# A fused attention and spectral mixer on one Trainium2 core: the last chunk's queries in two halves, one head of its last pack moved to ScalarE, chunk 13 normalised by block transposes

## The chip, the core and the metric

The kernel runs on one core of one Trainium2 chip. The metric is device time of one execution in microseconds (us); the time of a version is the median of its runs. The engines are TensorE (PE in the profile), VectorE (DVE), ScalarE (ACT), GpSimd (POOL) and SyncE (SP, which here only issues transfers).

## What is computed

The input `x` has 2048 tokens of 448 features. Two branches are mixed by a gate per token:

```python
g = sigmoid((x * gate_w).sum(-1, keepdims=True))
# a: attention with 16 heads of 28 features
q, k, v = split(x @ wqkv)
p = softmax(q k^T * 28 ** -0.5)
a = (p v, heads joined) @ wo
# b: spectral filter
b = irfft2(rfft2(x) * (w_r + 1j * w_i))
return g * a + (1 - g) * b
```

All tensors are bfloat16; the output is 2048 x 448.

## The kernel before

**Chunks and tiles.** Attention is worked off in 16 chunks, numbered `c`: four groups of four heads (`T = c // 4`) times four blocks of 512 queries (`qc = c % 4`). Chunk 15 is the last. A chunk has 16 key blocks of 128 keys, so it has 16 x 4 = 64 score pieces of 128 keys x 512 queries, and the whole kernel has 1024. TensorE makes a score piece in one of four strips of 32 rows, one strip per head (`score`, L820). Most pieces go to ScalarE, which takes the exponent of two or three at a time (`exp`, L1053; widths 1024 and 1536, in turns) into a tile `Pt`. The others go to VectorE in packs of one key block with four heads: `pack_step` (L834) writes each head as an integer, and `chain` (L849 to L883) makes the exponent of the four with six or seven further instructions. The seventh (L883) is used when the result is wanted soon; otherwise GpSimd issues a transfer that adds (L878).

**Values.** `pv` (L974) multiplies the exponents with the values of a key block: four TensorE matmuls side by side in four strips of 32 columns, accumulated over the 16 key blocks in one PSUM bank, `psPV`. The values carry a column of ones, so row 28 of each strip holds the softmax sum.

**Closing a chunk.** `close_chunk` takes `psPV` out. For chunks 0 to 13 VectorE copies it (L927), the sums go through four kinds of small transfers and back (L929, L942, L951), and GpSimd multiplies (L963). Chunks 14 and 15 use `turned` instead, on VectorE alone: a transpose in blocks of 32 x 32 (L1434), a reciprocal of the sums (L1435), a product with the gate (L1436), a product with the exponent sums' inverses (L1439) and a transpose back (L1441) into `oT`, from which TensorE takes the output projection. For chunk 15 the last two run twice, for the first and the second 256 queries.

**Output.** A token tile `t` has 128 tokens. `out_unit` (L769, L773) adds the spectral branch and the four groups of heads in a bank for the tiles 0 to 11; a copy (L779) and a transfer (L780) follow. Tiles 12 to 15 are the queries of chunks 3, 7, 11 and 15; all of them but chunk 15's part is made early (`base_unit`) and kept in fp32 (`late`). `finale` then adds chunk 15's part: for tiles 13 and 15 TensorE first loads the kept part into the bank by a product with an identity (fp32, L1457) and ScalarE copies the sum out (L1469), for tiles 12 and 14 VectorE adds it (`add_base`, L814). Four transfers write them (L815, L1470).

**Order.** Each engine works its own queue in the order in which the program issues; semaphores connect the queues. That order is made while the program is built, by a planner in `stream`: for each tile `k` of ScalarE it issues the exponent, then values that are ready (`do_pv`), then other TensorE work (`pick`, `step`), and then the scores of tile `k + 2`, all by estimated clocks for each engine (`tp` for TensorE, `tv` for VectorE, `ta` for ScalarE). `claim` decides which key blocks go to VectorE, `next_tile` what ScalarE gets. Where TensorE would have too little work, `until` and `dummy` put matmuls on zeros (`one_zero`, L1255; `zeros`, L1010). After the last exponent `tail` issues what is left, and `finale` the end.

Of the kernel before, what the change touches and what calls it, by code (L numbers as in the profile page):

```python
# [55 lines left out]
CLAIM, LAST = 10, 5  # L56
FIRST = 3
SOON = 18.1
STEPS, THIN = 3400, 3300
NV, NBASE = 10, 12  # L60
MOST = 7
LATE, LATE_END = 4, 5
BEGIN = 30.0
# [89 lines left out]
class Kernel:  # L153
# [19 lines left out]
    def setup(self):  # L173
# [77 lines left out]
        self.g32 = small("g32", [P, 2, NT], F32)  # L251
# [249 lines left out]
    def gate_unit(self):  # L501
# [21 lines left out]
        def ve(ps):  # L523
            nc.vector.tensor_copy(out=gT[:], in_=ps[0:2 * NT, 0:P])
            nc.vector.tensor_copy(out=gTb[:], in_=gT[:])
            nc.sync.dma_start(out=self.gD[:], in_=gT[0:NT])
            nc.sync.dma_start(out=self.hD[:], in_=gTb[NT:2 * NT])

            gv = self.gD[:]
            for h in range(4):  # L530
                nc.sync.dma_start(out=self.g16[32 * h:32 * h + 32, :, :],
                                  in_=_AP(tensor=gv.tensor, offset=gv.offset, ap=[[16, 32], [QW, 4], [1, 16]]))

            for h in range(4):
                nc.sync.dma_start(out=self.g32[32 * h:32 * h + 32, :, :],
                                  in_=_AP(tensor=gv.tensor, offset=gv.offset + 2 * QW, ap=[[1, 32], [QW, 2], [32, 16]]))
# [268 lines left out]
    def fin_unit(self, t):  # L805

        def ve(ps):
            self.add_base(ps, t, self.nc.sync)
        return Unit(f"fin{t}", [(lambda ps: self.out_pe(ps, t, (3,)), 0.30, 448, ve, 0.54)],
                    needs=[f"base{t}", f"oT{NC - 4 + t // 4}"])  # L810

# [6 lines left out]
    def score(self, out, c, i, h):  # L818
        T, qc = divmod(c, 4)
        self.nc.tensor.matmul(out, lhsT=self.kT[T][32 * h:32 * h + 32, 128 * i:128 * i + 128],  # L820
                              rhs=self.qT[T][32 * h:32 * h + 32, QW * qc:QW * qc + QW],
                              start=True, stop=True, tile_position=(32 * h, 0))

    def pack(self, c, i):

        return {"c": c, "i": i, "left": [0, 1, 2, 3], "t": None}
# [13 lines left out]
    def chain(self, c, i, t):  # L840
# [5 lines left out]

        def o1():
            st["n"] = self.rot1.tile([P, 4, QW], U16, name="n16")
            v.tensor_scalar(out=st["n"][:], in0=t[:], scalar1=511, scalar2=None, op0=ALU.bitwise_and)  # L849

        def o2():
            v.tensor_scalar(out=t[:], in0=t[:], scalar1=127 << 9, scalar2=2, op0=ALU.bitwise_and,  # L852
                            op1=ALU.logical_shift_right)

        def o3():
            st["a"] = self.rot2.tile([P, 4, QW], F16, name="pa16")
            v.tensor_scalar(out=st["a"][:], in0=st["n"][:], scalar1=C3 * k * k, scalar2=C2 * k,  # L857
                            op0=ALU.mult, op1=ALU.add)

        def o4():  # L860
            v.tensor_tensor(out=st["a"][:], in0=st["a"][:], in1=st["n"][:], op=ALU.mult)  # L861

        def o5():
            v.tensor_scalar(out=st["a"][:], in0=st["a"][:], scalar1=0.25 * k, scalar2=0.25 * (C1 * k + 1.0),  # L864
                            op0=ALU.mult, op1=ALU.add)

        soon = self.due(c) < SOON

        def done(at):
            self.pieces[(c, i)] = [t[:, h, :].bitcast(BF16) for h in range(4)]  # L870
            self.pack_t[(c, i)] = at

        def o6():
            q = st["a"][:] if soon else st["a"][:].bitcast(U16)
            v.tensor_tensor(out=q, in0=st["a"][:], in1=st["n"][:], op=ALU.mult)  # L875
            if not soon:

                nc.gpsimd.dma_start(out=t[:], in_=q, accum_op=ALU.add)  # L878
# [3 lines left out]
        def o7():  # L882
            v.tensor_tensor(out=t[:], in0=t[:], in1=st["a"][:], op=ALU.add)  # L883
            done(self.tv + VP + READY)
        for fn, cost, of in ((o1, E_TS, st), (o2, E_TS, None), (o3, E_TS, st), (o4, E_TT, st), (o5, E_TS, st),
                             (o6, E_TT, st)) + ((o7, E_TT, st),) * soon:
            self.vq.append((fn, cost, of))

    def due(self, c):

        return 4 * 0.447 * sum(len(self.free[n]) for n in range(self.act_c, c + 1) if n < NC)
# [23 lines left out]
    def close_chunk(self, c):  # L915
# [3 lines left out]
        if c == NC - 2:  # L919
            f = self.rot2.tile([P, NT, 32], F32, name="ot", tag="o32")  # L920
            z = self.rot2.tile([P, NT, 32], BF16, name="oz", tag="sqh")
            for part in self.turned(c, f, z, (0,)):
                self.dve(part)
# [32 lines left out]
        def scale():  # L956
            if c == 12:
                assert all(n in self.marks for n in ("k3.3", "q3.3", "f1.15"))
                self.oT.append(self.per.tile([P, S], BF16, name="oT3", tag="xT_oT3"))
# [9 lines left out]
    def pv(self, c, i, first, last):  # L969
        T = c // 4  # L970
        pcs = self.pieces.pop((c, i))
        self.packs -= self.pack_t[(c, i)] is not None
        for h in range(4):
# [69 lines left out]
    def exp(self, k):  # L1043
# [10 lines left out]
        for e, (c, i, h) in enumerate(self.tiles[k]):  # L1054
            self.pieces.setdefault((c, i), [None] * 4)[h] = Pt[:, e, :]
            if h == 3:
# [3 lines left out]
    def plan(self):  # L1060
        self.free = {c: list(range(NT)) for c in range(NC)}
        self.act_c, self.act_h, self.act_i = 0, 0, None
        self.epk = None
# [31 lines left out]
        m += [(0.0, self.out_unit(t)) for t in range(NBASE)] + [(0.0, self.fin_unit(t)) for t in range(NBASE, 12)]  # L1095
        self.mand = m

    def claim(self):
# [4 lines left out]
        for c, least in ((self.act_c + 1, NT - 4), (self.act_c, (LAST if self.act_c == NC - 1 else CLAIM) if self.act_c else FIRST)):  # L1103
# [4 lines left out]
            if len(self.free[c]) >= least and self.has(needs):  # L1108
                self.packs += 1
                return self.pack(c, self.free[c].pop(at))  # L1110

    def next_tile(self, k):

        t = []
        while len(t) < (2 if k % 2 else 3) and self.act_c < NC:
            if self.act_i is None:
                if not self.free[self.act_c]:
                    self.act_c += 1
                    continue
                self.act_i = self.free[self.act_c].pop(0)  # L1120
            t.append((self.act_c, self.act_i, self.act_h))
            assert self.act_c > 3 or {f"q0.{self.act_c}", f"k0.{self.act_i // 4}"} <= self.marks.keys()
            self.act_h = (self.act_h + 1) % 4
# [19 lines left out]
    def pick(self):  # L1143
# [6 lines left out]
        if banks:  # L1150
# [6 lines left out]
            for t, u in self.mand[-16:]:  # L1157
                if u.name[0:3] in ("out", "fin") and self.has(u.needs):
# [46 lines left out]
    def small(self, limit):  # L1205

        b = [i for i in (0, 1) if i not in self.open and self.bank_free[i] <= self.tp + 0.1]
        for _, u in self.mand:
            if b and u.name[0:3] == "fin" and self.has(u.needs):
                return self.step(u, b[0], limit)  # L1210
        return False

# [40 lines left out]
    def one_zero(self):  # L1253
        if self.pv_open:
# [4 lines left out]
        elif self.pv_c < NC and 2 not in self.open and self.tp >= self.pv_free:  # L1259
# [8 lines left out]
    def until(self, at):  # L1268

        while self.tp + E_MM <= at and self.thin(at) and self.one_zero():  # L1270
# [17 lines left out]
    def stream(self):  # L1288
# [4 lines left out]
        self.dummies = self.owed = 0  # L1293
        self.pv_c, self.pv_free, self.pv_open = 0, 0.0, False
# [18 lines left out]
        while self.ring:  # L1313
# [15 lines left out]
            while True:  # L1329
# [12 lines left out]
                if u is None or not self.step(*u, limit) and not self.small(limit):  # L1342
# [11 lines left out]
    def do_pv(self, k, left, most):  # L1354
        done = 0
        while done < most and self.pv_c < NC:
            c = self.pv_c
            if self.tp < self.pv_free or 2 in self.open:
                break
            cand = None  # L1360
            for i in sorted(left[c]):
                if not self.has([f"W{i // 4}" if c < 4 else f"V{i}"]):
                    continue
                if (c, i) not in self.pack_t:
                    continue
                t = self.pack_t[(c, i)]
                if t is None:
# [10 lines left out]
            first = len(left[c]) == NT  # L1378
            left[c].discard(cand)
            last = not left[c]  # L1380
            self.pv(c, cand, first, last)
# [4 lines left out]
            if last:  # L1386
                self.dve(0.75 if c == NC - 2 else 0.60, at=self.tp + PV)
# [5 lines left out]
                break  # L1393


    def tail(self):
# [8 lines left out]
        rest = sorted(left[c])  # L1405
        for i in rest:
            if i in rest[1:2]:

                for b, (u, _) in list(self.open.items()):
                    if len(u.phases) > 1:  # L1410
                        self.step(u, b, 1e9)
            self.pv(c, i, len(rest) == NT and i == rest[0], i == rest[-1])
        self.copy = nc.scalar.copy
        while self.open or len(self.mand) > 2 or any(u.name[0:3] != "fin" for _, u in self.mand):
            t = self.ready()
            assert t < 1e8, self.mand[0][1].name
            self.tp = max(self.tp, t)
            u = self.pick()
            if u:
                self.step(*u, 1e9)  # L1420
            else:
                self.tp += 0.2
            self.run_events()
        self.rest = [int(u.name[3:]) for _, u in self.mand]
        self.tail_left = [u.name for _, u in self.mand]

    def turned(self, c, f, z, parts):
# [4 lines left out]
        n = NT // len(parts)  # L1432
        i16 = self.rot2.tile([P, NT], F32, name="i16")
        v.transpose(out=f[:].rearrange("p j r -> p (j r)"), in_=self.psPV[:])  # L1434
        v.reciprocal(out=i16[:], in_=f[:, :, DH])  # L1435
        v.tensor_tensor(out=i16[:], in0=i16[:], in1=self.g32[:, qc - 2, :], op=ALU.mult)  # L1436
        for a in parts:
            zh = z[:, a:a + n, :]
            v.tensor_tensor(out=zh, in0=f[:, a:a + n, :], in1=with_free(i16[:, a:a + n], [[1, n], [0, 32]]), op=ALU.mult)  # L1439
            at = QW * qc + 32 * a  # L1440
            v.transpose(out=self.oT[T][:, at:at + 32 * n], in_=zh.rearrange("p j r -> p (j r)"))  # L1441
            yield 1.95

    def finale(self, psp):


        nc = self.nc
        v = nc.vector
        T, qc = divmod(NC - 1, 4)
        r = {n: psp.tile([P, n, QW], F32, name=f"ps{n}", tag=f"ps{n}", bufs=1) for n in ((3, 2) if self.N % 2 else (2, 3))}  # L1450
        bg = [psp.tile([P, QW], F32, name=f"bg{b}", tag=f"bg{b}", bufs=1) for b in (0, 1)]
        pf = [bg[0], r[3][:, 0], bg[1], r[2][:, 0]]
        eye = self.Fc[:, P + 8:P + 8 + P]
        for t, ps in zip(self.rest, (r[3][:, 1], r[2][:, 1])):
            self.out_pe(ps, t, (3,))
        for e in (1, 3):
            nc.tensor.matmul(pf[e][:, 0:D], lhsT=eye, rhs=self.base[4 * qc + e], start=True, stop=False)  # L1457
# [74 lines left out]
```

## Time and profile before

| | us |
|---|---|
| median of 3 runs (427.12 to 427.52) | 427.48 |
| the profiled execution, its own time | 426.82 |
| its span in the profile | 425.0 |
| busy: TensorE, ScalarE, VectorE | 408.4, 411.0, 395.3 |
| granted TensorE clock, mean | 1.0 |
| end of ScalarE's last exponent (L1053) | 417.07 |
| end of VectorE's last pack (L883) | 417.06 |
| issue of the last output transfers (L815, SyncE) | 421.72 to 422.59 |

The span runs from the first to the last instruction of the profiled execution; 1.82 us of its time lie around the span, and the median of the runs is 0.66 us above it. Times in a trace are counted from the span's start. In a row of the timeline the first number is the start, the second the length of the merged group; in a row of the chain of waits they are start and length of a step; in a row of the groups the busy time and the mean of one stand behind the bar.

### The profile page before, as it was taken

To read this page: it belongs to the slowest core of one execution; us is meant where nothing else is said; L and a number is where in the kernel's file an instruction comes from. 1 tells how busy PE (TensorE), PEld (TensorE's weight loads), DVE (VectorE), ACT (ScalarE), POOL (GpSimd) and SP (SyncE) were. 2 spreads that over 40 slices of the span, in tenths; PEclk is the share of its full clock that TensorE was granted. 3 is DMA by queue.
4 is the path that set the end of the run, shared out by engine and by line. 5 is a ranking of instruction groups with operands and counts; after the bars stand their busy time and mean duration, and the time that the engine had idled before them with its cause. 6 is when DMAs were issued, how large, how long until landed. Compare 5 with 4: busy or idle time off the path is not lost.

```text
span 425.0 us, 8196 instructions
## 1 busy us (share of the span) xinstructions
PE 408.4 (96%) x3139; PEld 144.9 (34%) x3139; DVE 395.3 (93%) x643; ACT 411.0 (97%) x369; POOL 50.3 (12%) x57
## 2 busy tenths in 40 slices
PE   9999999999999999999999999999999899999996
PEld 5343233333333333333333333333343233222331
DVE  6669889999989999999999999999999999999996
ACT  4999999999999999999999999999999999999994
POOL 6000002020110112011220100102002011201000
PEclk9999999999999999999999999999999999999999
DMA  9900200232302153375664446526453305240242
GB/s 242 211 11 2 7 27 13 64 60 43 77 15 47 24 97 62 74 166 103 159 148 95 104 103 134 96 68 110 108 149 77 76 2 106 54 107 29 57 99 75
DMA packets 30967, 35.08 MB, mean 83 GB/s; under 512 B 13296, under 2 KB 23536, under 8 KB 30896
## 3 DMA queue, kind: packets, MB, share of 16 engines
q1 hardware_dynamic: 26432, 20.48, 20.4%
q0 software_dynamic: 3744, 13.63, 17.5%
q8 instruction: 24, 0.39, 0.4%
q10 hardware_dynamic: 752, 0.44, 0.4%
q14 instruction: 15, 0.12, 0.1%
HBM read 15.10 MB, written 1.96 MB: 40 GB/s over the span
## 4 chain that ended last, share of the span: by engine, by line
PE 45%; ACT 25%; DVE 22%; issue 7%; ACTq 0%; DVEq 0%
ACT Pt L1053 21%; PE psPV L974 8%; PE ps L820 7%; DVE Pd L834 5%; PE bg L820 4%; PE psPV L1255 3%; PE bg L280 3%; PE bg L1010 3%; DVE pa L875 2%; PE bg L769 2%; PE bg L773 2%; DVE n L849 2%; DVE Pd L852 2%; DVE pa L861 2%; ACT early L1053 2%
## 5 line engine op out<-in xcount | busy, mean ns | idle before, releaser
L1053 ACT ACTIVATE Pt<-ps 128x1536 bf16<-128x1536 f32 x339 | 385.9, 1305 | 1.5 <-PE ps L820 0.6
L820 PE MATMUL ps<-qT,kT 32*128 32x512 bf16 x892 | 143.2, 382 | 4.3 <-ACT Pt L1053 2.8
L834 DVE TENSOR_SCALAR Pd<-bg 128x512 uint16<-128x512 f32 x132 | 90.0, 682 | 6.0 <-PE ps L820 4.2
L974 PE MATMUL psPV<-Pt,vsb 128*32 128x512 bf16 x832 | 81.1, 388 | 0.0
L820 PEld LDWEIGHTS <-kT 32*128 32x128 bf16 x1024 | 44.7, 91 | 95.1 <-issue 90.0
L820 PE MATMUL bg<-qT,kT 32*128 32x512 bf16 x132 | 50.6, 383 | 0.8 <-DVE Pd L834 0.3
L878 POOL DMA_DIRECT2D Pd<-pa x26 | 24.0, 924 | 214.7 <-PE ps L820 108.8
L1255 PE MATMUL psPV<-warm 128*128 128x512 bf16 x129 | 41.5, 385 | 0.0
L875 DVE TENSOR_TENSOR pa<-pa,n 128x2048 uint16<-128x2048 f16 (+1 forms) x33 | 40.9, 1240 | 0.5
L861 DVE TENSOR_TENSOR pa<-pa,n 128x2048 f16<-128x2048 f16 x33 | 40.9, 1239 | 0.3
L974 PEld LDWEIGHTS <-vsb 128*32 128x32 bf16 x1024 | 23.4, 93 | 52.0 <-issue 51.5
L1010 PE MATMUL bg<-warm 32*128 32x512 bf16 x92 | 35.2, 383 | 1.9 <-DVE Pd L834 1.8
L963 POOL TENSOR_TENSOR oT<-o,rep 128x512 bf16<-128x512 f32 x14 | 17.7, 1264 | 144.5 <-DVE oT L962 77.3
L280 PE MATMUL bg<-xT,Wg 128*128 128x512 bf16 (+1 forms) x112 | 29.6, 381 | 0.4
L852 DVE TENSOR_SCALAR Pd<-Pd 128x2048 uint16<-128x2048 uint16 x33 | 24.9, 755 | 0.3
L849 DVE TENSOR_SCALAR n<-Pd 128x2048 uint16<-128x2048 uint16 x33 | 22.9, 693 | 0.5
L864 DVE TENSOR_SCALAR pa<-pa 128x2048 f16<-128x2048 f16 x33 | 23.0, 698 | 0.0
L857 DVE TENSOR_SCALAR pa<-n 128x2048 f16<-128x2048 uint16 x33 | 22.5, 682 | 0.0
L671 DVE CAST U<-bg 128x450 bf16<-128x450 f32 x32 | 19.9, 621 | 2.0 <-PE bg L683 1.2
L1010 PEld LDWEIGHTS <-warm 32*128 32x128 bf16 x92 | 8.3, 91 | 28.8 <-issue 28.1
L769 PE MATMUL bg<-Binv,VT 128*128 128x448 bf16 x64 | 16.4, 355 | 0.1
L1255 PEld LDWEIGHTS <-warm 128*128 128x128 bf16 x131 | 9.5, 97 | 19.5 <-issue 17.9
(183 smaller groups left out, 430.0 us busy)
## 6 DMA issues: line engine op xcount, KB each, us to landing
Pd<-pa POOLq DMA_DIRECT2D x26, 512.0 KB, 4.8
rep<-rD SPq DMA_DIRECT2D x56, 64.0 KB
CR<-cRB SPq DMA_DIRECT2D x8, 256.0 KB
UT<-U SPq DMA_DIRECT2D x16, 112.5 KB
VT<-U SPq DMA_DIRECT2D x16, 112.5 KB
CR<-cCS SPq DMA_DIRECT2D x8, 192.0 KB
xtok<-in_A_x_dram SPq DMA_DIRECT2D x3, 448.0 KB
out_dram<-fin SPq DMA_DIRECT2D x12, 112.0 KB
```

The costliest lines, as they stand in the source:

```text
L280: self.nc.tensor.matmul(ps[:], lhsT=self.Wg[T, q][0:k, c, :], rhs=self.xT[0:k, c, 512 * b:512 * b + 512], start=(c == 0), stop=(c == 3))
L769: nc.tensor.matmul(ps[:, 0:D], lhsT=self.VT[:, t, 128 * (2 * fb + r):128 * (2 * fb + r) + 128], rhs=self.Binv[:, fb, r, :], start=(fb == 0 ...
L820: self.nc.tensor.matmul(out, lhsT=self.kT[T][32 * h:32 * h + 32, 128 * i:128 * i + 128], rhs=self.qT[T][32 * h:32 * h + 32, QW * qc:QW * q ...
L834: nc.vector.tensor_scalar(out=pk["t"][:, h, :], in0=ps[:], scalar1=SCALE * LOG2E * 512.0, scalar2=127.0 * 512.0, op0=ALU.mult, op1=ALU.add)
L849: v.tensor_scalar(out=st["n"][:], in0=t[:], scalar1=511, scalar2=None, op0=ALU.bitwise_and)
L852: v.tensor_scalar(out=t[:], in0=t[:], scalar1=127 << 9, scalar2=2, op0=ALU.bitwise_and, op1=ALU.logical_shift_right)
L861: v.tensor_tensor(out=st["a"][:], in0=st["a"][:], in1=st["n"][:], op=ALU.mult)
L875: v.tensor_tensor(out=q, in0=st["a"][:], in1=st["n"][:], op=ALU.mult)
L974: self.nc.tensor.matmul(self.psPV[32 * h:32 * h + 32, :], lhsT=self.vsb[:, i, 4 * T + h, :], rhs=pcs[h], start=first, stop=last, tile_posi ...
L1010: self.nc.tensor.matmul(ps[:], lhsT=self.warm[sl], rhs=with_free(self.warm[sl], [[0, 4], [1, P]]), start=True, stop=True, tile_position=(3 ...
L1053: self.nc.scalar.activation(out=Pt[:, 0:n, :], in_=ps[:, 0:n, :], func=ACT.Exp, scale=SCALE)
L1255: self.nc.tensor.matmul(self.psPV[:], lhsT=self.warm[:], rhs=with_free(self.warm[:], [[0, 4], [1, P]]), start=False, stop=False, skip_grou ...
```

## The change

Three things are altered, and the planner's order follows them.

1. **Chunk 13** is closed by `turned`, as chunks 14 and 15 are. The gate's table for it (`g32`) grows from two chunks to three.
2. **One head of the last pack.** Of the last key block that VectorE takes (of chunk 15) ScalarE gets one head (`MINE = 1`), and VectorE's chain works on 128 x 1536 instead of 128 x 2048.
3. **Halves.** The last two key blocks of chunk 15 that ScalarE gets are cut by queries: `split` makes eight entries, first the four heads of queries 0 to 255 with both key blocks side by side (part 0), then the four heads of queries 256 to 511 (part 1). Scores and values of these are 256 wide. When part 0's values are in, `pv_part` runs `turned` for it; the same for part 1. The new `tail` issues the output products of tiles 12 and 13 between the two parts. The last output tile's copy (L779) is taken by VectorE.

There are also new bounds for filling TensorE's waits with zeros (`LONG`, `FULL`), and `fin_unit` and `small`, which this configuration did not use, are gone. The core of the diff:

```diff
-CLAIM, LAST = 10, 5
+CLAIM, LAST = 10, 7
+TURN = 13
+SHARED, MINE = 1, 1
+PARTS = ((0, 256), (256, 256))
+SPLIT = 2
...
-        if c == NC - 2:
+        if c >= TURN:
...
+    def pv_part(self, i):
+        p = i[1]
+        ends = not any(j[1] == p for j in self.left[NC - 1])
+        self.pv(NC - 1, i, False, ends)
...
+        if ends:
...
+            self.turned(NC - 1, *self.ot, q0 // 32, w // 32)
...
+        for i in sorted(left[c], key=lambda i: (i,) if isinstance(i, int) else i):
+            if len(left[c]) == 1:
...
+                pf = [self.bank(b) for b in (0, 1)]
+                self.last_values(pf[0], 0, True)
+                self.sums(pf[1], 1)
+                self.last_values(pf[1], 1)
+                early = self.tv + 0.6 < self.ta + 0.7
...
+            if isinstance(i, int):
+                self.pv(c, i, not self.pv_open, not any(isinstance(j, int) for j in left[c]))
+            else:
+                self.pv_part(i)
...
+        self.sums(pf[2], 2)
+        self.last_values(pf[2], 2)
+        self.last_values(pf[3], 3, True)
```

`last_values` is the output projection of one token tile from `oT`, `sums` the fp32 product with the identity. The built program's TensorE queue ends so, weight loads left out (line numbers of the changed kernel; L990 and L985 are values, L1518 `last_values`, L1513 `sums`):

```
L990 psPV <- Pd 32x512  x4      a VectorE pack (waits for its transfer)
L990 psPV <- Pt 32x512  x1      the head that ScalarE took of the last pack
L990 psPV <- Pd 32x512  x3      the last VectorE pack (waits for VectorE)
L985 psPV <- Pt 32x256  x8      part 0 (the fourth waits for the last tile but one of ScalarE)
L1518 bg0 <- oT, Wo             tile 12 (its weight load waits for VectorE: part 0 normalised)
L1513 bg1 <- late, Fc           tile 13, fp32
L1518 bg1 <- oT, Wo             tile 13
L985 psPV <- Pt 32x256  x8      part 1 (waits for ScalarE's last tile)
L1513 ps2 <- late, Fc           tile 14, fp32
L1518 ps2 <- oT, Wo             tile 14 (waits for VectorE: part 1 normalised)
L1518 ps3 <- oT, Wo             tile 15
```

VectorE's queue ends with part 0's five instructions, part 1's five, and the additions for tile 12 and tile 15; ScalarE's with the copies for tiles 13 and 14.

## The prediction

> **What bounds the kernel now.** I began with the page's first two parts: TensorE 96%, ScalarE 97% and VectorE 93% busy, so no engine is free, but shares do not tell who ends last. So the timeline by engine of the last 60 us came next:
>
> ```profile
> 373.98 43.09 ACT L1053 ACTIVATE Pt<-ps 128x1024 bf16<-128x1024 f32 x38 [0.20 <-PE ps L820]
> ...
> 415.83 1.23 DVE L883 TENSOR_TENSOR Pd<-Pd,pa 128x2048 uint16<-128x2048 uint16 x1
> ...
> 417.28 0.40 PE L974 MATMUL psPV<-Pd,vsb 128*32 128x512 bf16 x4
> 417.50 0.39 PE L974 MATMUL psPV<-Pt,vsb 128*32 128x512 bf16 x4
> 417.82 0.55 PE L773 MATMUL bg<-Wo,oT 128*128 128x448 bf16 x2
> 418.21 1.67 PE L1457 MATMUL ps<-late,Fc 128*128 128x448 f32 x4
> ...
> 421.72 0.87 SPq L815 DMA_DIRECT2D out_dram<-U  x2
> ```
>
> ScalarE runs its 38 exponents without a gap worth naming to 417.07, 1.13 us each; VectorE ends its last pack at 417.06. Up to there the kernel is held by ScalarE, with VectorE equally late; after it 7.9 us remain. Note 417.50: two of those four value matmuls use exponents that were ready near 416.2 (the tile before ScalarE's last). They went after the four at 417.28, which had waited for L883: a waiting matmul holds what stands behind it. The chain of waits shows what the rest is made of:
>
> ```profile
> 417.35 0.57 PE psPV L974 x8
> ...
> 417.94 0.73 DVE ot L1434
> ...
> 418.69 0.26 DVE i L1435
> ...
> 419.19 0.43 DVE oz L1439
> ...
> 419.65 0.45 DVE oT L1441
> 420.10 0.32 DVE oz L1439
> ...
> 420.44 0.46 DVE oT L1441
> ...
> 420.94 0.36 PE bg L1463
> 421.30 0.20 PE ps L1463
> ...
> 421.53 0.53 ACT X L1469
> ```
>
> One pass of `turned` over 512 queries, then projection, copy and transfer. The fp32 product (L1457, 418.21 to 419.88) is not in the chain: it lies beside VectorE. The end is set by the last issue: the second L815, 422.59 - 0.39 = 422.20 (0.39 is ScalarE's one issue, L1470), 2.8 us before the span's end at 425.0.
>
> **Part by part.** *Chunk 13.* Removed: L927 0.68, the reciprocal L937 0.24 and product L938 0.17, memset L962 0.06: 1.15 us; added: 0.72 + 0.25 + 0.17 + 0.69 + 0.71 = 2.54 (the rows of chunk 14). VectorE works 1.39 us more. GpSimd's multiply (L963, 389.02 to 390.28) falls away; beside it an L852 took 1.40 us instead of 0.68, so 0.7 us come back. From SyncE's queue go the six transfers of chunk 13's sums (r, rD, four rep); nothing waits for a freer SyncE here. The wider `g32` reads half as many 4-byte elements more in its four transfers, issued from 48.78 to 51.42; the next issue is 55.76, so even 1.3 us more are covered. *One head.* VectorE loses one L834 (0.68) and a quarter of a chain: n, Pd, pa, pa, pa, pa, Pd = 0.69 + 0.68 + 0.68 + 1.22 + 0.68 + 1.22 + 1.22 = 6.39, a quarter 1.60. Against it two more output copies stand ahead of the last pack's end (12 instead of 10, 0.62 each). VectorE's net: 1.39 - 0.7 - 0.68 - 1.60 + 1.24 = -0.35, so the pack ends near 416.7; with the little slack that its queue has, 416.2 is possible. ScalarE's last tile is 1536 wide instead of 1024: 1.517 - 1.092 = 0.43 more (means of the two widths), end 417.50. That 0.43 I cost at nothing: TensorE is held elsewhere until after 420, below; were it not, the 0.43 would count in full.
>
> *Halves, scores and values.* The last three tiles' sixteen 256-wide scores stand in pairs on one strip, so a tile takes at most 6 x 0.11 = 0.66 instead of 0.22 (I halve the 0.22 between the two L974 groups). Between nothing and 0.4 a tile; I take nothing, since ScalarE works 0.91 to 1.36 meanwhile.
>
> *Halves, the end.* This part decides. Part 0's values need ScalarE's last tile but one (417.07 - 0.91 = 416.2) and stand behind the two packs. If VectorE's pack ends at 416.5: pack matmuls from 416.55, part 0 after 0.22, its two groups 0.11 + 0.28: done 417.15. Bounds are 416.7 (ScalarE alone) and 417.5 (pack as late as before, less the halved group).
>
> Now `turned` over 256 queries. These rows tell what half a width costs:
>
> ```profile
> L1434 DVE STREAM_TRANSPOSE ot<-psPV 128x512 f32<-128x512 f32 x2 | 1.4, 716 | 0.5 <-PE psPV L974 0.4
> ...
> L1441 DVE STREAM_TRANSPOSE oT<-oz 128x256 bf16<-128x256 bf16 x2 | 0.9, 446 | 0.1
> L1439 DVE TENSOR_TENSOR oz<-ot,i 128x256 bf16<-128x256 f32 x2 | 0.8, 404 | 0.0
> L1441 DVE STREAM_TRANSPOSE oT<-oz 128x512 bf16<-128x512 bf16 x1 | 0.7, 711 | 0.0
> ```
>
> A 256-wide transpose costs 0.446, not half of 0.711. No row has it in fp32: between 0.36 (half of 0.716) and 0.72; I take 0.45 by the bf16 ratio, since the 512-wide ones agree. One pass is 0.45 + 0.25 + 0.17 + 0.42 + 0.45 = 1.74, with five hand-overs of 0.03 to 0.04 1.92. Part 0 is normalised at 417.15 + 1.92 = 419.07.
>
> The new wait is on TensorE at tile 12's product. Behind it are queued tile 13's fp32 product and its projection, and then all of part 1's values, whose exponents are there at 417.50. From the rows: 0.05 until it starts, 0.20 for tile 12, 0.75 for one fp32 product (half of 1.67 less its last 0.16), 0.20 for tile 13, 0.10 for going over to column strips (0.32 against 0.22 at 417.50): 419.07 + 1.30 = 420.37. Part 1's eight matmuls 0.39: 420.76. VectorE, idle since 419.07, makes the second pass: 422.68. Tile 14's fp32 product lies beside that. Then 0.05 + 0.20 + 0.36 for tiles 14 and 15: 423.29. VectorE adds tile 15 (0.04 + 0.60): 423.93, issue 423.95 instead of 422.20: +1.75. By ScalarE's way (copy 0.53) its issue is at 423.65 instead of 422.09: +1.56. VectorE ends last. So the pass that ran once now runs twice in a row, 1.9 us each, against 2.95 from 417.94 to 420.89 before, and 1.7 us of TensorE work stand between the two.
>
> The span becomes 425.0 + 1.75 = 426.75, the profiled execution 428.57; the median of the runs shown is 0.66 above the profiled one, so 427.48 + 1.75 = **429.2 us**.
>
> **Rivals.** *The halves overlap as laid out, no change (not slower).* If TensorE gave part 1's values ahead of the blocked tile 12, they would be done at 417.50 + 0.05 + 0.39 = 417.95, the second pass would follow the first at once, 419.07 + 1.9 = 420.95, then 0.61 and 0.64: issue 422.22, +0.02, and 427.0 to 427.5 us with part 0's earliest start. It decides from part 1's values starting before 419. For it: the exponents are there. Against it: the queue order, and the row at 417.50, where ready matmuls stayed behind waiting ones. [...]
>
> *The earlier part of the last chunks gains.* Chunk 13's freer GpSimd and the lighter VectorE could feed ScalarE better. But the trace gives it 0.2 us of waiting in 43 us, and its pace, 2.27 us a pair, is that of the 66 exponents before (74.87 us). At most some tenths, 428.9; for "no change" 0.9 us would have to come from somewhere, which no row has. Losses are as possible: 0.4 a tile from the paired scores, though only the first two touch part 0, 429.6.
>
> *TensorE's clock falls in the gaps.* It now waits some 1.9 us at 417.15, and again before tile 14. The stretches of before:
>
> ```profile
> core 0: us, PE busy (x) PEld busy (x) DVE busy (x) ACT busy (x) POOL busy (x), PEclk, DMA share, GB/s
> ...
> 419.00:421.50 2.50, 1.98 (x7) 0.38 (x5) 2.40 (x7) 0.53 (x1) 0.00 (x0) 1.00 0.13 46
> 421.50:425.00 3.50, 0.00 (x0) 0.00 (x0) 0.46 (x1) 0.53 (x1) 0.00 (x0) 1.00 0.40 131
> ```
>
> The granted clock stays 1.00 through 3.5 us without a matmul. No row shows bursts between gaps, as they come now. At half speed (the first seven matmuls of the run, L303, take 3.15 / 7 = 0.45 each, later ones 0.22) a fall between the bursts adds 0.25 to part 1's values and 0.45 to the last two products: 429.9 us. [...]
>
> **How the numbers follow.** A measurement of this kernel can tell about 0.2%, 0.85 us, from no change. The sum as worked out, with part 0 between 416.7 and 417.5 and the fp32 transposes between 0.36 and 0.72 (two of them), is 428.6 to 429.8, chance 0.74; the clock 0.09; the overlap 0.07; gains upstream big enough for no change 0.06; a gain that no row shows 0.04. The range 428.3 to 430.0 leaves out the last three. Slower 0.84, same 0.12, faster 0.04.
>
> **What would show it.** Right: in the timeline after, L1528 to L1532 twice, with L1518, L1513, L1518 and part 1's L985 between; TensorE idle for nearly 2 us before L1518, released by VectorE's L1532; the last L817 issue near 424. Wrong: part 1's L985 near 417.6; the first L1528 after 418; ScalarE's last exponent far from 417.5; a granted clock below 1.

## The result, and the profile after

| | before | after |
|---|---|---|
| median (runs) | 427.26 us (6) | 429.57 us (6) |
| range of these runs | 426.72 to 427.52 | 428.49 to 429.78 |
| the profiled execution, its own time | 426.82 | 429.56 |
| its span | 425.0 | 427.8 |
| first main-stream mark on ScalarE (`ek`) | 25.77 | 26.93 |
| end of ScalarE's last exponent | 417.07 | 418.40 |
| from there to the end of the span | 7.95 | 9.35 |

The changed kernel is slower: ratio 1.0047, 95% interval 1.0036 to 1.0058. Of the 2.72 us between the two spans, 1.16 arise in the first 27 us, most of them because one tile of the input landed later (last section). To compare the rest, times are also counted from a fixed place after that: `ek`, ScalarE's one small exponent of width 64. From `ek` to the end of the span it is 399.26 us before and 400.82 after: **+1.56**. The exponents end 0.17 later (391.30 and 391.47 after `ek`), and what follows them takes 1.40 longer.

The chain of waits after, from part 0's values on (start, length, what; the late start of 1.16 is in every start):

```profile
417.73 0.30 PE psPV L985 x7
...
418.06 0.46 DVE ot L1528
...
419.44 0.46 DVE oT L1532
...
419.94 0.36 PE bg L1518
420.30 0.75 PE bg L1513 x2
421.05 0.19 PE bg L1518
421.24 0.36 PE psPV L985 x8
...
421.63 0.46 DVE ot L1528
...
423.01 0.46 DVE oT L1532
...
423.51 0.56 PE ps L1518 x2
...
424.10 0.62 DVE U L816
```

Before, one pass of `turned` stood in the chain (417.94 to 420.90) and the fp32 product not at all. Now VectorE runs the pass twice, 418.06 to 419.89 and 421.63 to 423.46, and four TensorE steps stand between the two: tile 12's projection, tile 13's fp32 product (0.75), its projection, and only then part 1's values, although ScalarE had finished their exponents at 418.40. The groups by shape in the same stretch give the half-wide fp32 row (L1528) that the profile before could only bound:

```profile
L1528 DVE STREAM_TRANSPOSE ot<-psPV 128x256 f32<-128x256 f32 x2 | 0.9, 449 | 2.5 <-PE psPV L985 2.5
L1532 DVE STREAM_TRANSPOSE oT<-oz 128x256 bf16<-128x256 bf16 x2 | 0.9, 445 | 0.1
```

The 2.5 us of idle time ahead of L1528 are VectorE waiting for values: 0.71 before the first pass, 1.75 before the second. The timeline of TensorE has the counterparts in brackets, 1.92 us before tile 12 and 0.99 before tile 14:

```profile
419.94 0.36 PE L1518 MATMUL bg<-Wo,oT 128*128 128x448 bf16 x1 [1.92 <-DVE oT L1532]
...
423.51 0.55 PE L1518 MATMUL ps<-Wo,oT 128*128 128x448 bf16 x2 [0.99 <-DVE oT L1532]
```

### The profile page after: what moved, and what is told of

Same layout as the page of the kernel before. It is cut to its first block, busy times and chain, and to the rows that moved or that the text cites. A ratio compares the mean times of both kernels' runs of the same rounds, so it can differ in the third digit from the quotient of the medians.

```text
span 427.8 us, 8197 instructions
## 1 busy us (share of the span) xinstructions
PE 406.9 (95%) x3134; PEld 145.6 (34%) x3153; DVE 395.6 (92%) x647; ACT 410.9 (96%) x368; POOL 50.2 (12%) x56
## 4 chain that ended last, share of the span: by engine, by line
PE 45%; DVE 22%; ACT 20%; issue 7%; DMA 5%; SPq 0%; ACTq 0%; DVEq 0%
ACT Pt L1069 18%; PE psPV L990 8%; PE ps L825 7%; DVE Pd L839 5%; PE bg L825 4%; PE psPV L1288 3%; PE bg L289 3%; DMA Bd<-cBd 3%; PE bg L1026 3%; PE bg L778 3%; PE bg L782 2%; DVE pa L883 2%; DMA xtok<-in_A_x_dram 2%; DVE Pd L860 2%; DVE n L857 2%
## 5 line engine op out<-in xcount | busy, mean ns | idle before, releaser
L825 PE MATMUL ps<-qT,kT 32*128 32x512 bf16 (+1 forms) x901 | 143.2, 380 | 4.1 <-ACT Pt L1069 2.8
L990 PE MATMUL psPV<-Pt,vsb 128*32 128x512 bf16 x825 | 80.7, 388 | 0.0
L883 DVE TENSOR_TENSOR pa<-pa,n 128x2048 uint16<-128x2048 f16 (+2 forms) x33 | 40.7, 1234 | 0.6
L990 PEld LDWEIGHTS <-vsb 128*32 128x32 bf16 x1016 | 23.4, 93 | 51.7 <-issue 51.2
L869 DVE TENSOR_TENSOR pa<-pa,n 128x2048 f16<-128x2048 f16 (+1 forms) x33 | 40.6, 1231 | 0.3
L971 POOL TENSOR_TENSOR oT<-o,rep 128x512 bf16<-128x512 f32 x13 | 16.4, 1264 | 135.2 <-DVE oT L970 66.9
L289 PE MATMUL bg<-xT,Wg 128*128 128x512 bf16 (+1 forms) x93 | 28.1, 381 | 1.2
L860 DVE TENSOR_SCALAR Pd<-Pd 128x2048 uint16<-128x2048 uint16 (+1 forms) x33 | 24.1, 730 | 0.4
L857 DVE TENSOR_SCALAR n<-Pd 128x2048 uint16<-128x2048 uint16 (+1 forms) x33 | 22.7, 689 | 0.4
L872 DVE TENSOR_SCALAR pa<-pa 128x2048 f16<-128x2048 f16 (+1 forms) x33 | 23.0, 697 | 0.1
L865 DVE TENSOR_SCALAR pa<-n 128x2048 f16<-128x2048 uint16 (+1 forms) x33 | 22.4, 679 | 0.0
L669 PE MATMUL bg<-Bd,xT 128*128 128x450 bf16 x64 | 15.6, 355 | 0.4
```

What stands on the lines that cost most here:

```text
L289: self.nc.tensor.matmul(ps[:], lhsT=self.Wg[T, q][0:k, c, :], rhs=self.xT[0:k, c, 512 * b:512 * b + 512], start=(c == 0), stop=(c == 3))
L825: self.nc.tensor.matmul(out[:, w * j:w * j + w], lhsT=self.kT[T][32 * h:32 * h + 32, 128 * i:128 * i + 128], rhs=self.qT[T][32 * h:32 * h ...
L857: v.tensor_scalar(out=st["n"], in0=t, scalar1=511, scalar2=None, op0=ALU.bitwise_and)
L860: v.tensor_scalar(out=t, in0=t, scalar1=127 << 9, scalar2=2, op0=ALU.bitwise_and, op1=ALU.logical_shift_right)
L869: v.tensor_tensor(out=st["a"], in0=st["a"], in1=st["n"], op=ALU.mult)
L883: v.tensor_tensor(out=q, in0=st["a"], in1=st["n"], op=ALU.mult)
```

## Experiments: the order at the end

Theory A: the loss is the order of TensorE's queue, which puts tiles 12 and 13 between the two passes. Theory B: the other parts of the change, chunk 13 and the head, delay the start or the main stream. The three kernels below and a repeat of the changed one shared a chip and 35 runs of the kernel before (427.28 us).

**fp32_first.** Tile 13's fp32 product goes ahead of tile 12's projection, into TensorE's idle time.

```diff
-                self.last_values(pf[0], 0, True)
                 self.sums(pf[1], 1)
+                self.last_values(pf[0], 0, True)
```

> Only tile 13's fp32 product is issued ahead of tile 12's product, so that it runs while TensorE waits for part 0; part 1's values stay behind both output products. Theory A: the second pass starts 0.75 us earlier, and the time is 0.75 us below the changed kernel, 0.9 above the kernel before; tail 8.65 us. Theory B gives the same tail and 1.2 us on the start. Rival: the two passes of VectorE are the cost, not what stands between them; then no change.

Measured: 427.64 us, ratio 1.0008 (0.9991 to 1.0024). The end takes 8.60 us instead of 9.35: exactly the 0.75 of the fp32 product. In the timeline the product (L1513) has left the space between the passes:

```profile
416.58 1.02 PE L1513 MATMUL bg<-late,Fc 128*128 128x448 f32 x2
418.58 0.55 PE L1518 MATMUL bg<-Wo,oT 128*128 128x448 bf16 x2 [0.98 <-DVE oT L1532]
419.06 0.40 PE L985 MATMUL psPV<-Pt,vsb 128*32 128x256 bf16 x8
```

**part1_first.** Part 1's values and pass are issued ahead of tiles 12 and 13.

```diff
-                self.last_values(pf[0], 0, True)
-                self.sums(pf[1], 1)
-                self.last_values(pf[1], 1)
...
                 self.pv_part(i)
+        self.last_values(pf[0], 0, True)
+        self.sums(pf[1], 1)
+        self.last_values(pf[1], 1)
```

> The output products of tiles 12 and 13 (with the fp32 product) are issued behind part 1's values instead of ahead of them; nothing else. Theory A: part 1's values start when part 0's first transpose has read the bank, some 0.5 us after part 0's values, VectorE's second pass follows the first at once, the 1.75 us of idle time before it are gone; about 1.6 us less than the changed kernel, within 0.3 us of the kernel before, tail 7.8 us. Theory B: the tail shortens all the same, but the start stays late: 1.2 us above the kernel before. Rival of theory A (TensorE is not what holds VectorE): no change against the changed kernel.

Measured: 426.63 us, ratio 0.9981 (0.9963 to 0.9999). The end takes 7.67 us, 1.68 less than in the changed kernel and 0.28 less than before. VectorE's second pass follows its first at once:

```profile
418.07 0.45 DVE L1530 STREAM_TRANSPOSE oT<-oz 128x256 bf16<-128x256 bf16 x1
418.44 0.41 DVE L1526 STREAM_TRANSPOSE ot<-psPV 128x256 f32<-128x256 f32 x1
```

One rearrangement of TensorE's queue takes the whole loss away, and halves, head and chunk 13 are all still there. The idle time is gone with it: what VectorE waited for was the queue order, not the exponents.

**no_halves.** Chunk 13's transposes and the moved head stay; the last two key blocks are taken whole, and `tail` and `finale` are those of before.

```diff
-            if self.act_c == NC - 1 and self.act_i is None and len(self.free[NC - 1]) == SPLIT and not self.extra:
+            if False:
                 self.split()
```

> The halves are undone (no split; all values 512 wide; one pass of the transposes over 512 queries with the projection by halves as in the kernel before); chunk 13 by transposes and the head on ScalarE stay. Theory A: the halves are the whole loss; within 0.3 us of the kernel before: the last tile 0.43 us wider on ScalarE, VectorE's last pack earlier; tail 7.6 us, since the values wait for ScalarE alone. Theory B: 1.2 us above the kernel before, from the start. If chunk 13 or the head cost something by themselves, ScalarE's last exponent comes later than 417.07 + 0.43 (head of the run deducted).

Measured: 426.86 us, ratio 0.9991 (0.9972 to 1.001), the end 7.95 us as before, `ek` to the end 399.39. So the halves, in the order in which they were queued, are the whole loss, and the other two parts together change nothing that can be measured.

**after_again.** The changed kernel once more.

> The changed kernel as it is, beside the others. Its profile had two differences: from ScalarE's last exponent to the span's end 9.40 us (418.40 to 427.8) instead of 7.93, and ScalarE's exponent of ek at 26.93 instead of 25.77, so 1.16 us lost in the first 26 us. Theory A (the end): the head's 1.16 us come and go between executions and have nothing to do with the change; here the time is 1.75 us above the kernel before, the tail again 9.4 us. Theory B (the start): the change itself delays the start, the exponent of ek is again near 26.9, here and in every kernel that keeps the change's other parts, and the time is 1.5 + 1.2 - 0.4 = 2.3 us above or more.

Measured: 429.33 us, ratio 1.0041 (1.0022 to 1.0061), the end 9.35 again, `ek` to the end 400.80. But its single executions fall apart: four at 428.25 to 428.43, the others up to 430.99. The chain's 1.56 us explains the lowest; the median lies 0.5 us above that (427.28 + 1.56 = 428.84), and the late start is not in every execution. That was the question for the next runs.

## Experiments: the two other parts, and the spread

**no_turn** closes chunk 13 the old way (`TURN = 14`), halves and head as in the change.

> The changed kernel with chunk 13 closed as before (copy, transfers, GpSimd's product); halves and the moved head stay. If chunk 13's block transposes cost VectorE what the sum took (1.39 less GpSimd's 0.7 of hold-up, hidden by the other work), the end stays as in the changed kernel: 7.95 + 1.4 = 9.3 us behind ScalarE's last exponent, 429.2 to 429.6. If they are what lets the last packs end sooner, VectorE or ScalarE end later without them: 430 to 430.5. If they are part of the loss: 428.8 or less, and an earlier start of the first long exponents too.

Measured: 429.22 us, ratio 1.0038 (1.0021 to 1.0056). The end takes 9.29 us, as in the first case, but ScalarE ends 391.94 after `ek` instead of 391.47, and the first pass starts 0.73 later; `ek` to the end is 401.22, +0.40. The second case holds for ScalarE alone. VectorE's last pack ends sooner without chunk 13's transposes, 389.32 after `ek` instead of 390.42, and VectorE then waits for values:

```profile
414.02 0.96 DVE L891 TENSOR_TENSOR Pd<-Pd,pa 128x1536 uint16<-128x1536 uint16 x1
...
417.52 0.45 DVE L1528 STREAM_TRANSPOSE ot<-psPV 128x256 f32<-128x256 f32 x1 [2.02 <-PE psPV L985]
```

So with the transposes VectorE's pack comes later, two more output copies standing ahead of it, as the sum had it; the end still comes about 0.4 us sooner in the trace, by way of ScalarE and of part 0's values. The planner orders everything after chunk 13 anew, so this pair of traces does not show which of its moves does it. The median does not show the gain, for a reason that comes below.

**no_head** leaves the last pack whole on VectorE (`SHARED = 0`).

> The changed kernel with no head of the last pack moved to ScalarE; halves and chunk 13's transposes stay. The sum gave VectorE 0.68 + 1.60 us less to do by the head, against 0.43 more for ScalarE. If part 0 waits for VectorE's pack, as the sum had it, part 0's first transpose comes up to 1.6 us later, the whole end with it, 430 to 431 us, while ScalarE's last exponent ends about 0.4 sooner after the start. If VectorE has slack there, no later than the changed kernel: 428.9 to 429.6.

Measured: 432.1 us, ratio 1.0102 (1.0073 to 1.0131), more than either case. ScalarE ends 0.39 sooner (391.08 after `ek`), as expected; the first pass starts 1.94 later (393.07 instead of 391.13), so part 0 does wait for VectorE's pack, and moving the head brings far more than it costs ScalarE. But `ek` to the end is 404.11, +3.29: another 1.35 came from somewhere. The stretches of this kernel tell from where (after the bounds: length, then TensorE, weight loads, VectorE, ScalarE and GpSimd busy, granted clock, DMA share, GB/s):

```profile
417.57:420.98 3.41, 0.62 (x12) 0.23 (x11) 2.55 (x6) 0.00 (x0) 0.00 (x0) 1.00 0.00 0
420.98:424.39 3.41, 3.11 (x13) 1.16 (x14) 0.33 (x2) 0.53 (x1) 0.00 (x0) 0.50 0.00 0
```

For 3.41 us the granted clock is 0.50, right through tiles 12 and 13 and part 1's values. All four runs of this kernel have a mean clock of 0.989 to 0.993.

**after_last** is the changed kernel again.

> The changed kernel once more, last of its call (it was first before). In its two profiled executions the first exponents of the main stream began 0.7 and 1.2 us later than in the other kernels, 26.5 and 26.9 instead of 25.6 to 25.8. If that belongs to the program: the same again, median 429.3 to 429.6. If it belongs to the place in the call or to chance: start near 25.7 and the median near 428.8, that is 427.28 + 1.55, the loss from the start on.

Measured: 429.44 us, ratio 1.0045 (1.002 to 1.007). The profiled execution started early (`ek` at 25.60), so the late start does not belong to the program. Its end, however, took 9.89 us instead of 9.35. From 419.89 on the stretches are cut where the trace's record of the clock changes, and the first is as long as the second:

```profile
416.48:419.89 3.41, 1.48 (x15) 0.53 (x12) 1.69 (x5) 0.60 (x1) 0.00 (x0) 1.00 0.00 0
419.89:423.30 3.41, 3.26 (x13) 0.73 (x12) 2.20 (x6) 0.83 (x2) 0.00 (x0) 0.50 0.11 34
423.30:426.71 3.41, 0.04 (x1) 0.00 (x0) 0.62 (x1) 0.24 (x1) 0.00 (x0) 1.00 0.30 101
```

In the first row TensorE is busy for 1.48 of 3.41 us, because the gap of 1.93 us lies wholly inside; the second row has the clock at 0.50; the third has it back at 1.00. In the profile of the change shown first the gap is as long, 1.92 us, and the granted clock stays at 1.00 from 6.16 to 426.00:

```profile
415.76:419.17 3.41, 2.25 (x27) 0.70 (x25) 2.56 (x6) 2.64 (x3) 0.00 (x0) 1.00 0.12 36
419.17:422.58 3.41, 2.58 (x14) 0.91 (x14) 1.53 (x6) 0.53 (x1) 0.00 (x0) 1.00 0.00 0
```

There, too, the 3.41 us that lie about the gap as the first row of after_last does (417.80 to 421.21) hold only 1.49 us of TensorE work, and no fall follows; what makes one execution fall and the other not is not shown by these traces.

By TensorE's waits at the end the profiles stand so: in no_head, with 2.29 us (for VectorE's pack) and 1.94, the clock falls to 0.50 at 420.98; in the changed kernel, with 1.92 to 1.93, it falls ahead of the last product in one profile of four; in no_turn (1.45), fp32_first (0.98 and 0.99) and part1_first (0.55 and 0.98) it stays at 1.00 up to the last product.

The single executions agree: a mean clock of 0.996 or less in 15 of 31 of the changed kernel, 4 of 4 of no_head, and none of no_turn's 10, fp32_first's 12 and part1_first's 12. That fits with no_turn's median, which shows no loss although its chain is longer. That the gaps bring the low clocks stays short of shown, for three reasons. The kernel before has so low a mean in 29 of 87 executions, though TensorE waits no longer than 0.27 us ahead of its last products (L1463), so a low mean alone does not show a fall in the gap. Only one of four profiles of the changed kernel caught a fall. And one fall of 3.41 us (1.7 us of clock, 0.004 of the span) with the fall behind the last product (at most some 0.002) hardly reaches the eleven executions that lie at 0.992 to 0.994; what else lowered the clock in them is not shown.

**filled** tests whether the gaps bring the low clocks: the changed kernel with products of zeros in TensorE's two gaps.

```diff
+                for _ in range(7):
+                    self.zero(pf[1], self.tp)
                 self.last_values(pf[0], 0, True)
...
         self.sums(pf[2], 2)
+        for _ in range(3):
+            self.zero(pf[3], self.tp)
         self.last_values(pf[2], 2)
```

> The changed kernel with TensorE's two gaps at the end filled by products of zeros that nothing reads: seven (128x512, about 0.22 each) between part 0's values and tile 12's product, three between tile 14's fp32 product and tile 14's projection. Order and data of all other work stay. In after_last the granted clock fell to 0.50 at 419.89 for 3.41 us, after a stretch of 3.41 us in which TensorE had idled 1.93, and the end took 9.89 us behind ScalarE's last exponent instead of 9.35. [...]

Measured: 428.47 us, ratio 1.0031 (1.0016 to 1.0046); the end 9.35 us. TensorE's two waits are down to 0.31 and 0.34 us, and the granted clock stays at 1.00 through the end:

```profile
416.70:420.11 3.41, 3.10 (x26) 1.38 (x26) 2.01 (x6) 1.39 (x2) 0.00 (x0) 1.00 0.00 0
420.11:423.52 3.41, 3.07 (x18) 0.92 (x16) 2.08 (x6) 0.53 (x1) 0.00 (x0) 1.00 0.11 34
```

Eleven of the 12 executions have a mean clock of 0.997 or more, one 0.996, while the kernel before, run beside it, had 0.995 or less in 11 of 23. The median is 0.9 us below the changed kernel's 429.3 to 429.6, with nothing taken out of the chain; but the changed kernel did not run beside it, and the intervals of the ratios still overlap, so it is the clocks, 1 of 12 low against 15 of 31, that speak for the gaps as the cause. Four executions lie above 429.3, one more reason for which shows in the profiled one (429.40): a late start, `ek` at 26.63.

**after_look** and **before_look** are one more profiled execution each, of the changed kernel and of the kernel before.

> The changed kernel, one profiled execution more. Of its 30 executions so far 15 have a mean clock of 0.996 or less, ten of them 0.992 to 0.994, which is more than the one fall of 3.41 us that after_last shows. [...]

Measured: 428.23 us, clock 0.998, `ek` at 25.62, the end 9.36 us. TensorE waits 1.92 and 0.99 us, as in the profile shown first, and its work behind the gap is not slowed: the eight value products take 0.40 us as a group, the two passes of tile 14's fp32 product 1.02. This is the change undisturbed, as the chain has it.

> The kernel before, one profiled execution more. A third of its executions have a mean clock of 0.993 to 0.995, with 427.4 to 428 us instead of 426.7 to 427.3. [...]

Measured: 427.31 us, clock 0.998, the end 7.96 us; no execution with a low clock was caught. What lowers the mean clock in 29 of 87 executions of the kernel before (median 427.76 against 427.17 for the others) stays open. In its first profile TensorE waits 0.27 and 0.23 us at the end, and the granted clock is 1.00 up to the span's end.

## Two versions beyond

**best** changes part1_first's order: tile 12 is made by an fp32 product too, which makes three, and those of tiles 13 and 12 go ahead of the projections. **fp32_both_first** puts those of tiles 13 and 14 there, beside VectorE's passes. Its edit against part1_first:

```diff
-        self.last_values(pf[0], 0, True)
-        self.sums(pf[1], 1)
-        self.last_values(pf[1], 1)
...
+        self.sums(pf[1], 1)
         self.sums(pf[2], 2)
+        self.last_values(pf[0], 0, True)
+        self.last_values(pf[1], 1)
         self.last_values(pf[2], 2)
```

> Part 1's values ahead of everything else, as in part1_first, and TensorE's late work put in another order: the fp32 products of tiles 13 and 12 while VectorE makes part 0's pass, then both projections, then the fp32 product of tile 14, then tile 15 and tile 14. Tiles 12, 13 and 14 are copied by ScalarE, only tile 15 is added by VectorE. In part1_first tile 14's fp32 product ended at 420.46, 0.3 after VectorE's last transpose (420.2), and VectorE's last addition began at 421.04. Theory A (what counts is what stands between the two passes, and then the order behind them): the last addition begins near 420.55, the stretch from ScalarE's last exponent to the end is 7.2 to 7.4 us instead of 7.67, about 426.3 us, ratio 0.997 to 0.998. Rival (the transfers' own time sets the end, whatever was issued when): 7.6 to 7.7 us, 426.6.

> part1_first with tile 14's fp32 product moved ahead too: both fp32 products (tiles 13 and 14) lie beside VectorE's first pass, then the projections of tiles 12 to 15 in order; VectorE adds tiles 12 and 15, ScalarE copies 13 and 14. In part1_first VectorE's last transpose ended at 420.23 and its last addition began at 421.04, since tile 14's fp32 product held TensorE until 420.46; best had three fp32 products and came to the same 0.46 of waiting. Theory A (what is left is TensorE's fp32 work behind the second pass): the last addition begins near 420.75, tail 7.35 to 7.45 instead of 7.67, about 426.35 us, ratio 0.997 to 0.998. Rival (the end is held by the transfers): tail 7.6 to 7.7, 426.6.

Measured: 426.62 us, ratio 0.998 (0.9965 to 0.9995), end 7.59; and 426.59 us, ratio 0.998 (0.9967 to 0.9993), end 7.52. Both beat the kernel before by about 0.2%, and neither part1_first by what can be measured. The end is 0.08 and 0.15 shorter than in part1_first, where 0.27 to 0.47 and 0.22 to 0.32 were expected, so best comes out at the rival's 7.6 to 7.7 and fp32_both_first between the two. The rival's reason does not hold for fp32_both_first: the last addition begins 3.83 after ScalarE's last exponent (421.02) instead of 4.00 in part1_first, and of these 0.17 us the end gains 0.15. In best the last addition is earlier still (420.80, 3.65 after), but ScalarE's copy of tile 14 ends at 421.52, and its transfer is issued last. In fp32_both_first TensorE now waits 0.61 us for VectorE's second pass, so the passes themselves are what is left there, not the fp32 work.

## Why the prediction was right, step by step

- **The sum.** +1.75 was forecast, +1.56 measured from `ek` on. Two errors partly cancel: up to the end of the last addition the sum is 0.37 too late (423.93 against 424.72 - 1.16 = 423.56), and from there to the end of the span 0.21 too short (2.82 against 3.03). after_look, with an early start and the full clock, took 428.23 us; the forecast for the profiled execution was 428.57. That the median came as near as 429.57 to the 429.2 is in part luck: the chain alone gives 427.26 + 1.56 = 428.82, and what lies above it are late starts and falls of the clock, of which the sum had none. Two figures at the prediction's end do not follow from its parts: with part 0 at 417.5 and both fp32 transposes at 0.72 the sum is 430.1, not 429.8, and the chances add up to 0.83 for slower and 0.13 for same.
- **Part 0's values.** Taken at 417.15 within 416.7 to 417.5; measured, with the late start's 1.16 taken off, 418.03 - 1.16 = 416.87. VectorE's pack ended at 417.35 - 1.16 = 416.19, the early one of the two ends given. no_head shows that it is the pack that sets this: 1.94 us, against 0.68 + 1.60 in the sum.
- **The row at 417.50.** The prediction read it as ready matmuls behind waiting ones. But L883 ended at 417.06, and what held the four at 417.28 was TensorE's own work, as the chain of before shows:

```profile
416.86 0.48 PE bg L773 x2
417.35 0.57 PE psPV L974 x8
```

That ready matmuls stay behind a waiting one is shown by the change instead: part 1's exponents were there at 418.40, and its values came at 421.24, behind tiles 12 and 13.

- **The pass.** 1.92 forecast, 1.83 measured, both times; the fp32 transpose of 256 was taken at 0.45 and is 0.449. The reciprocal (0.20 instead of 0.25) and shorter hand-overs make the difference.
- **Between the passes.** 1.30 + 0.39 = 1.69 forecast, 419.89 to 421.57 = 1.68 measured, the fp32 product of 0.75 confirmed by taking it away.
- **ScalarE.** The 0.43 was costed at nothing, and that held: its last exponent ended at 418.40, 2.84 ahead of part 1's turn on TensorE (421.24). no_head prices the head at 0.39 on ScalarE; its end moved by only 0.17, and no_turn shows chunk 13's transposes giving it 0.47 back. That the sum did not have: it booked chunk 13 as 1.39 of VectorE work less 0.7. 0.39 - 0.47 is not 0.17; the 0.25 between stays open.
- **The overlap rival.** Out in the change, and real in part1_first, where the order allows it: 427.0 to 427.5 was forecast for it, 426.63 measured. The two halves cost nothing by themselves; their place in TensorE's queue is what costs.
- **The clock rival.** Its chance of 0.09 was low. "The granted clock stays 1.00 through 3.5 us without a matmul" holds for that stretch alone: the record of before has the clock at 0.50 from 425.49 on, just behind the span's end at 425.0, and in after_last a fall to 0.50 comes 1.27 us behind a gap of 1.93 us. The rival came true in one of the four profiles and, by the mean clocks, in up to half of the executions (15 of 31; a low mean alone does not show it). Its price was near: 0.25 for part 1's values and 0.45 for the last two products forecast; after_last starts its second pass 0.22 to 0.25 later than the other three profiles of this kernel (394.92 against 394.67 to 394.70 after `ek`) and ends 0.54 later. Executions with a mean clock over 0.996 have a median of 428.71, the others 429.70, late starts in both; so the median of 429.57 is the chain's +1.56 and, in part of the executions, this and the late start.

## What to carry to other kernels

When work is cut in halves to overlap, write down the queue of each engine between the halves: whatever waits for the first half's result blocks the second half's inputs on the same queue, ready or not (here part 1's values, whose exponents were there at 418.40 and which came at 421.24). A chain with gaps can have a second price on TensorE: with a gap of 1.92 to 1.93 us one profile of four here ran 3.41 us of the end at a granted clock of 0.50, and the end took 0.54 us longer. Ten products of zeros left one low mean clock in 12 here, an order with shorter gaps (fp32_first and part1_first, 0.99 us at most) none in 24.

## What the runs showed of the hardware that was not expected

- The granted clock differs between executions of one program. The changed kernel, run in turn on one chip (after_again), gives 428.25 us at a mean clock of 0.997 and 429.65 at 0.994, and of its four profiles one shows a fall ahead of the last product and three none. The mean clock does not tell everything: filled took 429.40 us at 0.999, with a late start (`ek` at 26.63).
- A fall ahead of the last product lasted 3.41 us in both profiles that show one (after_last, no_head) and lengthened what TensorE had in it: in after_last the two passes of tile 14's fp32 product took 1.86 us as a group instead of 1.02, and eight value products 0.62 instead of 0.40.
- A late start: in the changed kernel's first two profiles TensorE waited 0.72 and 0.42 us, near 10.5 us, for a part of the input (`xtok`), and ScalarE, between its first long exponents, 1.02 and 0.73. It came and went with the same program (`ek` at 26.93, 26.46, 25.60 and 25.62), and why the transfer was late stays open. Of the 1.16 us in the first of these profiles, 0.23 lie ahead of that wait: the first scores start at 8.94 instead of 8.71, and the trace's record of the clock begins, at 1.00, at 6.16 instead of 5.66.
